# Two half passes over the first two blocks, and x taken from PSUM by column groups

## The chip, the cores and the metric

The kernel runs on one core of a Trainium2 chip. The metric is the device time of one execution in microseconds; the median of three runs of the kernel before is 1110.03.

## The reference

Per batch and head a linear attention with a complex decay runs over 768 positions (B = 4, H = 8, D = 48), and its output goes through two layers of 384 -> 2048 -> 384:

```python
mag = np.sqrt(a_re * a_re + a_im * a_im)
scale = np.minimum(mag, 0.999) / (mag + 1e-06)
for t in range(S):                       # a = (a_re + i a_im) * scale
    S_re = ar * S_re - ai * S_im + k[t] (x) v[t]
    S_im = ar * S_im + ai * S_re         # with the old S_re
    y[t] = q[t] @ S_re
x = y as (B * S, H * D)
x = (h * cos(h)) @ w_out,   h = x @ w_in
out = elu(h) @ w2_out,      h = x @ w2_in
```

The weights arrive as 64-bit floats, and the kernel decodes them on the chip.

## The kernel before, in words

The positions are cut in 6 chunks of 128, and with 4 batches that gives 24 steps; step i is (chunk i // 4, batch i % 4). A step of the attention takes logarithm and angle of the decay (`a1_pre`, `a1_ln`, `a1_lam`, `a1_th`), sums them over the chunk with a triangular product (`p_tri`), makes exponentials, cosine and sine (`a2_exp`, `a2_ph`, `a2_trig`), scales q and k with them (`a2_mag`, `a2_xy`), transposes the two results four heads at a time (`b_tr`), forms masked scores (`b_sc`), y from scores and from the state of the chunks before (`b_y`), and the new state (`b_ds`). y comes out transposed, heads in rows, in one bank of PSUM. `b_out` copies it to SBUF, six DMAs regroup its rows to three full blocks of 128, and `x_split` cuts it into a rounded part (ScalarE) and a rest (GpSimd).

Three steps are one block of 384 columns. The first layer runs 8 blocks of 16 units; a unit is one slice of 128 hidden rows: nine products into h (L467), a chain over ScalarE, VectorE and GpSimd (`chain_a`, `chain_b`, `chain_c`), and nine products that add to the block's three accumulators (L568). The second layer does the same for 8 blocks of the layer's result, with its own weights. A unit's h is formed three units ahead of its last products (LA).

Weights of the first layer: `w_load` brings a slice as 64-bit words, `w_dec` turns it into 32-bit floats (one scaling on ScalarE, L435, three operations on VectorE, L436 to L439), `w_put` splits it (a cast on ScalarE, L452, a subtraction on VectorE, L454). Those of the second layer are decoded during blocks 4 to 6 of the first and stored.

What sets the order: ScalarE executes in the order in which the code emits its instructions. For the other engines a scheduler orders by priority, which starts as the order of emission and is shifted by `prio` (OFF for decoding, OFP for `w_put`, PRI per token). The opening is a written list of tokens, PRO: the attention of steps 0 to 2, parts of the next ones, and R, D, P for loading, decoding and putting one weight. After it the three first units start, and the steps that follow come in eight pieces each (SLOT; a number after the colon is an offset to the step), spread over the units of a block so that a block's three steps are ready before it starts (`need`, `run_pieces`). SP issues all DMAs in one queue. PSUM has eight banks: three accumulators, five working banks (`work`) for everything else.

For the general case the kernel checks bounds of a_re and a_im (`bounds`): for steps 9 and later in `a1_pre`, for the first NDF = 9 in the second layer from a second load.

Of the kernel before, what the change touches and what calls it, by code (L numbers as in the profile page):

```python
# [11 lines left out]
F32 = mybir.dt.float32  # L12
# [18 lines left out]
OFF = (-200, 0)  # L31
# [3 lines left out]
YTA, RHP, CARP = 3, 2, 0  # L35
NDF = 9
# [6 lines left out]
NYT, NXS = 2, 2  # L43
NX, PD = 4, 23
PRO = ('L:0 L:1 L:2 R pre:0 pre:1 V:0 Q:1 V:2 V:1 Q:2 R Q:0 pre:2 TL ln:0 ln:1 ln:2 lam:0 lam:1 lam:2 TT th:0 th:1 th:2 D P TL tri:0 tri:1 exp:0 tri:2 exp:1 exp:2 R ph:1 TT ph:0 ph:2 D trig:0 P trig:1 mag:2 trig:2 mag:0 xy:0 mag:1 R tr0:0 xy:1 xy:2 D R L:3 tr1:0 P sc0:0 tr0:1 D sc1:0 tr1:1 y0:0 tr0:2 R sc1:1 D sc0:1 y1:0 P out:0 ds:0 y0:1 sc0:2 Q:3 y1:1 tr1:2 sc1:2 pre:3 V:3 R out:1 D ds:1 y0:2 P y1:2 ln:3 lam:3 L:4 R out:2 ds:2 xs:1 TT ca:3 pre:4 th:3 tri:3 xs:0 ca:4 D P xs:2 ln:4 L:5 exp:3 lam:4 P ph:3 th:4 trig:3 V:4 mag:3 xy:3 Q:4')
# [8 lines left out]
def tile_kernel(ctx, tc, q, k, v, a_re, a_im, w_in, w_out, w2_in, w2_out, out):  # L54
# [17 lines left out]
    xp = ctx.enter_context(tc.tile_pool(name="xp", bufs=2))  # L72
# [10 lines left out]
    def work():  # L83
        return psW.tile([P, 512], F32, tag="work", name="work")

    def prio(x):
# [20 lines left out]
    Sst = [ap.tile([D2, H, D], F32, name=f"S{b}", tag=f"S{b}") for b in range(B)]  # L107
# [5 lines left out]
                cs=(1, 0), q=(1, 2), k=(1, 3), Y=(2, 0), v=(2, 2), r=(2, 3))  # L113
# [13 lines left out]
    def load(i, names):  # L127
        c, b = steps[i]
        for nm in names:
            t = buf(i, nm, LB[nm]).rearrange("p (h d) -> p h d", h=H)  # L130
            nc.sync.dma_start(out=t, in_=SRC[nm][b, :, c * P:(c + 1) * P, :].rearrange("h t d -> t h d"))
            st[i][nm] = t
# [19 lines left out]
    def a1_pre(i):  # L152
# [7 lines left out]
        e = buf(i, "e")  # L160
        if i >= NDF:
            bounds(i, ar, ai)
        s["L"], s["w"], s["e"] = L, w, e

    def a1_ln(i):
        s = st[i]
        if i >= NB0:
            nc.scalar.preload_act_table_set(LN_SET)  # L168
        ar, e = fl(s["ar"]), s["e"]
# [10 lines left out]
    def a1_lam(i):  # L180
        s = st[i]
        L = s["L"]
        nc.vector.scalar_tensor_tensor(out=L, in0=L, scalar=2.0 * LN_CAP, in1=s["w"], op0=ALU.min,
                                       op1=ALU.subtract)
        if i >= N_NAT:
            s["hi"] = ap.tile([P, 2, HD], F32R, name="lth")
            s["lo"] = ap.tile([P, 2, HD], F32R, name="ltl")
            split(s["hi"][:, 0, :], s["lo"][:, 0, :], L)

    def a1_th(i):  # L190
        s = st[i]
        th = s["th"]
        nc.scalar.activation(out=th, in_=th, func=AF.Arctan, scale=-1.0)
# [14 lines left out]
    def p_tri(i):  # L208
        s = st[i]
        s["Lp"], s["Fp"] = work(), work()  # L210
        if i < N_NAT:
            nc.tensor.matmul(out=s["Lp"][:, 0:HD], lhsT=tri, rhs=s["L"], start=True, stop=True)
            nc.tensor.matmul(out=s["Fp"][:, 0:HD], lhsT=tri, rhs=s["th"], start=True, stop=True)
            return
        for j, ps in ((0, s["Lp"]), (1, s["Fp"])):
            nc.tensor.matmul(out=ps[:, 0:HD], lhsT=tri_r, rhs=s["hi"][:, j, :], start=True, stop=False)  # L216
            nc.tensor.matmul(out=ps[:, 0:HD], lhsT=tri_r, rhs=s["lo"][:, j, :], start=False, stop=True)  # L217

    def a2_exp(i):
# [37 lines left out]
    def a2_mag(i):  # L257
        s = st[i]
        for m, x in (("E", "q"), ("En", "k")):
            nc.gpsimd.tensor_tensor(out=fl(s[x]), in0=s[m], in1=fl(s[x]), op=ALU.mult)  # L260

    def a2_xy(i):
        s = st[i]
        for nm, m, eng in (("X", "q", nc.vector), ("Y", "k", nc.gpsimd)):
# [5 lines left out]
    def b_tr(i, g):  # L270
        s = st[i]
        for nm, on in (("X", "XT"), ("Y", "YT")):
            ps = work()
            for h in range(4):
                nc.tensor.transpose(ps[0:D2, h * P:(h + 1) * P],  # L275
                                    s[nm][:, g * 4 + h].rearrange("p a d -> p (a d)"), ident)
            t = ap.tile([D2, 4, P], F32, name=on, bufs=2 if nm == "X" else NYT)
# [17 lines left out]
    def w64(h):  # L295
        return slice(min(h * D, HD - 64), min(h * D, HD - 64) + 64)

    def b_y(i, g):
# [4 lines left out]
        yp = s["yp"]  # L303
        for pr in range(2):
            gp = g * 2 + pr
            for n in range(2):
                hh = pr * 2 + n
                nc.tensor.matmul(out=yp[n * 64:n * 64 + 64, gp * P:(gp + 1) * P], lhsT=fl(s["v"])[:, w64(g * 4 + hh)],  # L308
                                 rhs=s["AT", g][:, hh, :], start=True, stop=c == 0)
            if c > 0:  # L310
                for n in range(2):
                    hh = pr * 2 + n
                    nc.tensor.matmul(out=yp[n * 64:n * 64 + 64, gp * P:(gp + 1) * P],  # L313
                                     lhsT=fl(Sst[b])[:, w64(g * 4 + hh)], rhs=s["XT", g][:, hh, :],
                                     start=False, stop=True)
# [18 lines left out]

    def b_out(i):
        s = st[i]
        if i < NB0:
            yT = scr[3 * i][:, 2:4, :].rearrange("p a f -> p (a f)")[:, 0:4 * P]
            yT = yT.rearrange("p (a t) -> p a t", a=4)
            xs = buf(i, "E").rearrange("p (a t) -> p a t", a=KT)  # L340
        else:
            yT = ap.tile([P, 4, P], F32, name="yT")
            xs = ap.tile([P, KT, P], F32, name="xs", bufs=NXS)
        nc.scalar.copy(out=yT.rearrange("p a t -> p (a t)"), in_=s["yp"])
        s["xs"] = xs
        dm = nc.sync.dma_start
        dm(out=xs[0:48, :, :], in_=yT[0:48, 0:3, :])
        dm(out=xs[48:96, :, :], in_=yT[64:112, 0:3, :])
        dm(out=xs[96:128, 0, :], in_=yT[0:32, 3, :])
        dm(out=xs[96:112, 1, :], in_=yT[32:48, 3, :])  # L350
        dm(out=xs[112:128, 1, :], in_=yT[80:96, 3, :])
        dm(out=xs[96:128, 2, :], in_=yT[96:128, 3, :])
# [17 lines left out]
    def x_split(i):  # L370
# [3 lines left out]
        split(xh[:, :, sl], xl[:, :, sl], st[i]["xs"])  # L374

    TOK = dict(L=lambda i: load(i, ("ar", "ai")), Q=lambda i: load(i, ("q", "k")), V=lambda i: load(i, ("v",)),
               pre=a1_pre, ln=a1_ln, lam=a1_lam, ca=a1_carry, th=a1_th, sp=a1_sp, tri=p_tri, exp=a2_exp, ph=a2_ph,
               trig=a2_trig, mag=a2_mag, xy=a2_xy, tr0=lambda i: b_tr(i, 0), tr1=lambda i: b_tr(i, 1),
               sc0=lambda i: b_sc(i, 0), sc1=lambda i: b_sc(i, 1), y0=lambda i: b_y(i, 0), y1=lambda i: b_y(i, 1),
               ds=b_ds, out=b_out, xs=x_split,  # L380
               TL=lambda i: nc.scalar.preload_act_table_set(LN_SET),
               TT=lambda i: nc.scalar.preload_act_table_set(TRIG_SET),
# [453 lines left out]
```

## Time and profile before

| | |
|---|---|
| median of three runs | 1110.03 us (1109.04 to 1110.41) |
| the profiled execution's own time | 1111.97 us |
| its span in the trace | 1110.3 us |
| busy: TensorE, ScalarE, VectorE, GpSimd | 1033.3, 768.6, 631.7, 547.8 us |
| mean granted clock of TensorE | 0.97 |

The span is what lies between the first and the last instruction of the trace. The page gives each engine's busy time over all of it; the rows below cut it at the blocks of the first layer. A line number in a row is one of the kernel before; where a helper emits an instruction, it is the helper's line (L146 is the subtraction in `split`). PE is TensorE, DVE VectorE, ACT ScalarE, POOL GpSimd.

### The profile page before, as it was taken

The numbers are of one execution on the slowest core, as the hardware profiler recorded it, in microseconds if no ns is written. First come the engines' busy times: TensorE is split into PE (matmuls) and PEld (weight loads), VectorE is DVE, ScalarE is ACT, GpSimd is POOL, SyncE is SP. The second block draws the span as 40 slices with busy tenths as digits, with TensorE's granted clock in tenths as the row PEclk, the third lists the DMA queues.
The fourth block names the chain that finished last, engine by engine and source line by source line (L and its number), as shares of the span: only waits on it lengthen the run. The fifth ranks groups of instructions, "written<-read, shape, count | busy, mean of one in ns | idle before, by whom it ended". The sixth has DMA issues, their size and how long they took to land.

```text
span 1110.3 us, 18114 instructions
## 1 busy us (share of the span) xinstructions
PE 1033.3 (93%) x6498; PEld 982.2 (88%) x6498; DVE 631.7 (57%) x999; ACT 768.6 (69%) x1492; POOL 547.8 (49%) x471
## 2 busy tenths in 40 slices
PE   2567987999999999899999999999999999999997
PEld 1456877999999999789899899999999999999997
DVE  3867897665574774786887565434333334333332
ACT  6677866777786875776877456876666767666664
POOL 2435565565555573573665346783434344343432
PEclk9778997999999999899999999999999999999999
DMA  9553551232232322654544275320000010100000
GB/s 204 131 145 68 123 130 30 52 64 59 50 62 48 66 51 58 185 136 121 152 125 154 81 190 136 114 65 22 22 23 22 22 43 1 44 1 22 1 22 26
DMA packets 199037, 85.19 MB, mean 77 GB/s; under 512 B 164573, under 2 KB 190745, under 8 KB 198937
## 3 DMA queue, kind: packets, MB, share of 16 engines
q1 hardware_dynamic: 198936, 83.94, 30.0%
q8 instruction: 53, 0.87, 0.3%
q14 instruction: 48, 0.39, 0.1%
HBM read 63.40 MB, written 15.79 MB: 71 GB/s over the span
## 4 chain that ended last, share of the span: by engine, by line
PE 79%; ACT 5%; DVE 3%; issue 1%; POOL 1%; DMA 0%; SPq 0%; ACTq 0%; DVEq 0%; POOLq 0%
PE work L467 34%; PE acc L568 27%; PE work L568 6%; PE work L288 3%; PE work L275 2%; PE work L308 2%; PE work L313 1%; PE work L324 1%; ACT L168 1%; PE work L216 1%; DVE dec L436 1%; DVE dec L437 1%; DVE wt L454 1%; POOL xl L146 0%; PE work L217 0%
## 5 line engine op out<-in xcount | busy, mean ns | idle before, releaser
L467 PE MATMUL work<-xh,wt 128*128 128x384 f32 x1536 | 444.7, 345 | 14.0 <-DVE wt L454 5.2
L146 POOL TENSOR_TENSOR gl<-t,gh 128x384 fp32r<-128x384 f32 x256 | 279.4, 1094 | 297.0 <-ACT gh L145 118.4
L467 PEld LDWEIGHTS work<-xh,wt 128*128 128x128 f32 x1536 | 283.4, 191 | 24.9 <-DVE wt L454 6.9
L467 PE MATMUL work<-xl,wt 128*128 128x384 f32 x768 | 224.2, 339 | 0.1
L524 DVE SCALAR_TENSOR_TENSOR t<-e,t 128x384 f32<-128x384 f32 x128 | 76.6, 598 | 229.8 <-ACT t L523 161.4
L568 PE MATMUL acc<-gh,wt 128*128 128x384 f32 x768 | 201.9, 350 | 0.1
L145 ACT CAST gh<-t 128x384 fp32r<-128x384 f32 x256 | 130.2, 509 | 92.3 <-PE acc L568 58.1
L568 PE MATMUL acc<-wt,gh 128*128 128x384 f32 x512 | 161.8, 334 | 0.0
L467 PEld LDWEIGHTS work<-xl,wt 128*128 128x128 f32 x768 | 143.5, 191 | 0.4 <-POOL xl L146 0.4
L568 PEld LDWEIGHTS acc<-gh,wt 128*128 128x128 f32 x768 | 139.4, 193 | 3.6 <-issue 2.9
L517 ACT ACTIVATE t<-work 128x384 int32<-128x384 f32 x128 | 61.6, 481 | 80.1 <-PE work L467 74.8
L534 DVE TENSOR_TENSOR t<-work,t 128x384 f32<-128x384 f32 x128 | 70.6, 551 | 66.1 <-ACT t L533 65.4
L568 PE MATMUL acc<-gl,wt 128*128 128x384 f32 x384 | 103.2, 340 | 4.4 <-POOL gl L146 4.4
L518 DVE SCALAR_TENSOR_TENSOR t<-t,work 128x384 f32<-128x384 int32 x128 | 69.8, 546 | 51.1 <-ACT t L517 50.2
L568 PEld LDWEIGHTS acc<-wt,gh 128*128 128x128 f32 x512 | 95.3, 188 | 0.0
L521 ACT ACTIVATE t<-work 128x384 f32<-128x384 f32 x128 | 62.8, 491 | 33.3 <-PE work L467 24.9
L568 PE MATMUL work<-wt,gh 128*128 128x384 f32 x256 | 85.5, 334 | 0.0
L533 ACT ACTIVATE t<-t,hpi 128x384 f32<-128x384 f32 x128 | 78.8, 616 | 3.8 <-DVE t L518 3.7
L568 PE MATMUL acc<-wt,gl 128*128 128x384 f32 x256 | 76.4, 334 | 0.0
L568 PEld LDWEIGHTS acc<-gl,wt 128*128 128x128 f32 x384 | 69.7, 190 | 5.5 <-POOL gl L146 5.4
L536 DVE SCALAR_TENSOR_TENSOR t<-work,t 128x384 f32<-128x384 f32 x128 | 71.4, 558 | 4.4
L522 ACT ACTIVATE e<-t 128x384 f32<-128x384 f32 x128 | 67.4, 527 | 4.1
(142 smaller groups left out, 1748.0 us busy)
## 6 DMA issues: line engine op xcount, KB each, us to landing
raw<-in_moe_w_out_dram SPq DMA_DIRECT2D x32, 384.0 KB
raw<-in_moe_w_in_dram SPq DMA_DIRECT2D x16, 384.0 KB
w2f<-dec SPq DMA_DIRECT2D x16, 384.0 KB
raw<-w2f SPq DMA_DIRECT2D x16, 384.0 KB
raw<-in_moe_w_in_dram SPq DMA_DIRECT2D x16, 288.0 KB
x2d<-ev SPq DMA_DIRECT2D x24, 192.0 KB
x2s<-x2d SPq DMA_DIRECT2D x8, 576.0 KB
out_dram<-ev SPq DMA_DIRECT2D x24, 192.0 KB
```

The lines of the kernel that those rows point to most:

```text
L145: nc.scalar.copy(out=hi, in_=x)
L146: nc.gpsimd.tensor_tensor(out=lo, in0=x, in1=hi.bitcast(F32), op=ALU.subtract)
L467: nc.tensor.matmul(out=out_ps, lhsT=a, rhs=b_, start=m == 0, stop=m == n - 1)
L517: nc.scalar.activation(out=ki, in_=h, func=AF.Copy, scale=1.0 / TWO_PI, bias=0.25)
L518: nc.vector.scalar_tensor_tensor(out=t, in0=ki, scalar=-TWO_PI, in1=h, op0=ALU.mult, op1=ALU.add)
L521: nc.scalar.activation(out=t, in_=h, func=AF.Relu, scale=-1.0)
L522: nc.scalar.activation(out=e, in_=t, func=AF.Exp, scale=-1.0)
L524: nc.vector.scalar_tensor_tensor(out=t, in0=e, scalar=1.0, in1=t, op0=ALU.add, op1=ALU.mult)
L533: nc.scalar.activation(out=t, in_=t, func=AF.Sin, bias=hpi)
L534: nc.vector.tensor_tensor(out=t, in0=h, in1=t, op=ALU.mult)
L536: nc.vector.scalar_tensor_tensor(out=t, in0=h, scalar=0.0, in1=t, op0=ALU.max, op1=ALU.add)
L568: nc.tensor.matmul(out=o, lhsT=a, rhs=b_, start=ff == 0 and x == 0, stop=ff == NFF - 1 and x == 2)
```

## The change

1. Units: block 0 and block 1 run slices 0 to 7 in turn, then slices 8 to 15 in turn. At the end of a first half the accumulators are stored to x2d; near the end of the second half they are loaded and added. Weights are paced over 18 units, and the pieces of the steps follow the new order.
2. y in groups of 32 columns: four heads' first or last 32 columns go to the four quarters of the output rows, and the 16 that remain of two heads share a group, padded by zeros, so that y is in PSUM as three full blocks of 128. `x_split` reads PSUM directly, its rest on VectorE. `b_out` and its six DMAs are gone; w_in's rows are loaded in the matching order.
3. `table` writes a load of ScalarE's function table only where the last one differs.
4. Engines: the first five weights are scaled and cast on VectorE (ED); q and k are scaled on VectorE in the first five steps (MG); Y is formed on VectorE in the first three (YG) and evicted on VectorE in all (YTA); the product with a_im is on VectorE always (RHP).
5. All 24 bounds are checked in the second layer (NDF), in its blocks 1 and 2.
6. The token list PRO and the pieces SLOT are rewritten; transposes and their evictions are separate tokens (tr, ev), as are the two prefix products (tl, tf). OFF for the second layer's decoding goes from 0 to -200.

```diff
-OFF = (-200, 0)
+OFF = (-200, -200)
-YTA, RHP, CARP = 3, 2, 0
-NDF = 9
+YTA, RHP, CARP = 0, 0, 0
+NDF = 24
+MG, YG = 5, 3
-PRO = ('L:0 L:1 L:2 R pre:0 pre:1 V:0 Q:1 V:2 V:1 Q:2 R Q:0 pre:2 TL ln:0 ...
+PRO = ('Q:2 L:1 L:0 V:1 L:2 V:0 R Q:0 R pre:1 Q:1 pre:0 ln:0 D pre:2 ln:1 ln:2 lam:0 lam:1 lam:2 tl:0 tl:1 tl:2 exp:0 exp:1 th:0 th:2 P L:3 exp:2 R mag:1 R tf:0 th:1 ph:0 tf:1 ph:1 mag:0 trig:0 xy:0 D tr0:0 tf:2 trig:1 tr1:0 ph:2 ev0:0 ds:0 ev1:0 xy:1 sc0:0 tr0:1 sc1:0 y0:0 tr1:1 trig:2 mag:2 y1:0 ev0:1 xy:2 xs:0 sc0:1 ev1:1 V:2 sc1:1 y0:1 y1:1 tr0:2 tr1:2 ds:1 ev0:2 ev1:2 D D sc1:2 pre:3 P sc0:2 xs:1 y0:2 ln:3 lam:3 y1:2 ds:2 xs:2 D th:3 P tf:3')
-SLOT = ['out:-1 tri:1 pre:2', 'L:3 ln:2 tr0 ph:1 exp:1', 'sc0 xs:-1 tr1 lam:2', 'trig:1 ca:2', 'mag:1 y0 th:2', 'sc1 xy:1 V:2 sp:2', 'Q:2 y1', 'ds']
+SLOT = ['xs:-1 pre:2', 'tl:1 tf:1 exp:1 ph:1 tr0 ev0 ln:2', 'tr1 sc0 y0 lam:2 ev1 trig:1', 'sl:2 L:3 sc1 mag:1',
+        'ca:2', '', 'th:2', 'Q:2 sp:2 y1 xy:1 ds V:2']
+FA, NXB, ED, P0 = 8, 3, 5, 1
+WS = 18
...
+    def table(name):
+        if tab[0] != name:
+            nc.scalar.preload_act_table_set(name)
+            tab[0] = name
...
+    def wide32(t, h):
+        x = (h % 2) * 16
+        return fl(t)[:, h * DP + x:h * DP + x + 32]
+    def rest32(t, h):
+        x = h * DP + (32 if h % 2 == 0 else -16)
+        return fl(t)[:, x:x + 32]
...
+        for kind in range(1 if c == 0 else 2):
+            for j in range(4):
+                h = 4 * g + j
+                a, x = ((V, s["AT", g]), (Spad[b], s["XT", g]))[kind]
+                nc.tensor.matmul(out=yp[32 * j:32 * j + 32, g * P:(g + 1) * P], lhsT=wide32(a, h), rhs=x[:, j, :],
+                                 start=kind == 0, stop=kind == 1 or c == 0)
+        if g == 0:
+            return
+        for kind in range(1 if c == 0 else 2):
+            for n in range(2):
+                for j in range(4):
+                    h = 2 * j + n
+                    a, x = ((V, s["AT", h // 4]), (Spad[b], s["XT", h // 4]))[kind]
+                    nc.tensor.matmul(out=yp[32 * j:32 * j + 32, 2 * P:3 * P], lhsT=rest32(a, h), rhs=x[:, h % 4, :],
+                                     start=kind == 0 and n == 0, stop=n == 1 and (kind == 1 or c == 0))
...
-        split(xh[:, :, sl], xl[:, :, sl], st[i]["xs"])
+        yp = st[i]["yp"][:, 0:HD].rearrange("p (m t) -> p m t", m=KT)
+        nc.scalar.copy(out=xh[:, :, sl], in_=yp)
+        nc.vector.tensor_tensor(out=xl[:, :, sl], in0=yp, in1=xh[:, :, sl].bitcast(F32), op=ALU.subtract)
...
+            trip = cols.rearrange("(m t r) f -> m t r f", t=3, r=32)
+            for m in range(2):
+                for n in range(2):
+                    keep(nc.sync.dma_start(out=raw[64 * n:64 * n + 64, 0, m], in_=trip[2 * m + n, 0:3:2]))
+            keep(nc.sync.dma_start(out=raw[:, 0, 2], in_=trip[:, 1]))
...
-    units = [(0, j, ff) for j in range(NBK) for ff in range(NFF)]
+    segs = [(0, 0, 0, FA), (0, 1, 0, FA), (0, 0, FA, NFF), (0, 1, FA, NFF)]
+    segs += [(0, j, 0, NFF) for j in range(2, NBK)]
+    units = [(l, j, ff) for l, j, a, b_ in segs for ff in range(a, b_)]
...
+    def part_load(j):
+        c0, n = blocks[j][0] * P, ncols(0, j)
+        part[j] = t = stg.tile([P, KT, HD], F32, tag="raw", name="part")
+        nc.sync.dma_start(out=t[:, :, 0:n], in_=x2d[:, :, c0:c0 + n])
...
+                nxt = max([f for a, b_, f in units[:g + LA + 1]]) + 1
+                tgt = min(max(nxt, w00 + (NFF - w00) * (g + 1) // WS), NFF)
                 w_adv(0, tgt + WL)
                 p_adv(0, tgt)
```

## Rows read from the trace of the kernel before

**Rows 1.** Stretches cut at the first layer's blocks: per engine busy us (instructions), clock.

```profile
core 0: us, PE busy (x) PEld busy (x) DVE busy (x) ACT busy (x) POOL busy (x), PEclk, DMA share, GB/s
0.00:76.02 76.02, 32.57 (x209) 23.02 (x209) 46.26 (x62) 49.50 (x84) 23.61 (x25) 0.85 0.77 161
76.02:185.40 109.38, 91.76 (x525) 80.92 (x525) 92.51 (x127) 82.76 (x149) 65.52 (x45) 0.85 0.43 98
185.40:259.50 74.10, 74.10 (x530) 69.50 (x530) 44.89 (x77) 53.98 (x107) 40.17 (x36) 1.00 0.26 53
259.50:335.40 75.90, 75.90 (x541) 71.37 (x540) 47.69 (x80) 55.78 (x111) 44.51 (x40) 1.00 0.27 56
335.40:411.40 76.00, 76.00 (x542) 71.47 (x541) 48.25 (x80) 55.85 (x111) 44.65 (x41) 1.00 0.27 56
411.40:493.60 82.20, 78.78 (x543) 73.80 (x542) 56.98 (x90) 58.24 (x114) 45.68 (x38) 0.96 0.43 114
493.60:574.90 81.30, 77.43 (x528) 72.40 (x527) 63.34 (x96) 60.82 (x119) 46.75 (x40) 0.98 0.50 144
```

**Rows 2.** TensorE's waits, 0 to 200 us: who waited for whom, total, times, longest.

```profile
PE work L212 <- DVE scr L183: 15.1, 1, 15.1
PE work L275 <- DVE scr L267: 8.3, 1, 8.3
...
PE work L467 <- DVE wt L454: 5.2, 2, 2.9
```

**Rows 3.** ScalarE in order of time: start, us, operation, idle time before it.

```profile
64.63 0.57 ACT L344 COPY scr<-work 128x512 f32<-128x512 f32 x1
...
68.36 1.28 ACT L382 ACT_TABLE_LOAD   x1
...
75.45 0.51 ACT L145 CAST xh<-scr 128x384 fp32r<-128x384 f32 x1 [1.18 <-DMA scr<-scr]
```

**Rows 4.** TensorE in order of time, the layer's first product.

```profile
76.02 4.21 PE L467 MATMUL work<-xh,wt 128*128 128x384 f32 x12 [1.97 <-ACT xh L145]
```

**Rows 5.** ScalarE by line, 0 to 76 us: busy, mean ns, idle before.

```profile
L435 ACT ACTIVATE dec<-raw 128x768 f32<-128x768 f32 x7 | 6.4, 909 | 0.0
L452 ACT CAST wt<-dec 128x768 fp32r<-128x768 f32 x6 | 5.0, 827 | 11.1 <-DVE dec L439 11.1
```

**Rows 6.** VectorE by line and shape, 0 to 76.02 us.

```profile
L437 DVE SCALAR_TENSOR_TENSOR dec<-raw,dec 128x768 int32<-128x768 int32 x7 | 6.7, 954 | 0.2
L267 DVE TENSOR_TENSOR scr<-scr 128x768 f32<-128x768 f32 x3 | 6.0, 2017 | 0.0
L436 DVE TENSOR_SCALAR dec<-dec 128x768 int32<-128x768 int32 x7 | 5.8, 823 | 8.4 <-ACT dec L435 8.4
...
L454 DVE TENSOR_TENSOR wt<-dec,wt 128x768 fp32r<-128x768 f32 x6 | 5.7, 953 | 2.1 <-ACT wt L452 2.1
```

**Rows 7.** VectorE by line and shape, 76.02 to 185.4 us.

```profile
L454 DVE TENSOR_TENSOR wt<-dec,wt 128x768 fp32r<-128x768 f32 x11 | 13.7, 1242 | 0.7 <-ACT wt L452 0.7
...
L437 DVE SCALAR_TENSOR_TENSOR dec<-raw,dec 128x768 int32<-128x768 int32 x9 | 11.2, 1246 | 0.1
```

**Rows 8.** VectorE by line and shape, 259.5 to 335.4 us.

```profile
L281 DVE COPY YT<-work 96x512 f32<-96x512 f32 x7 | 4.8, 686 | 1.0 <-PE work L275 1.0
...
L267 DVE TENSOR_TENSOR X<-cs,q 128x768 f32<-128x768 f32 x3 | 2.9, 954 | 0.6 <-POOL gl L146 0.6
...
L177 DVE TENSOR_TENSOR ai<-th,ai 128x384 f32<-128x384 f32 x1 | 0.5, 549 | 0.0
```

**Rows 9.** TensorE in order of time: score products, transposes; two groups of y products.

```profile
233.32 1.06 PE L288 MATMUL work<-XT,YT 96*128 96x128 f32 x8
234.21 0.60 PE L275 MATMUL work<-ident,X 128*96 128x128 f32 x4
...
244.99 0.39 PE L313 MATMUL work<-XT,S 96*64 96x128 f32 x4
245.21 0.39 PE L308 MATMUL work<-AT,v 128*64 128x128 f32 x4
```

More of the change, by code (lines that the diff above doesn't have):

```diff
@@ L106, in tile_kernel @@
     ap = att.enter_context(tc.tile_pool(name="ap", bufs=1))
-    Sst = [ap.tile([D2, H, D], F32, name=f"S{b}", tag=f"S{b}") for b in range(B)]
+    DP = D + 16
+    Spad = [ap.tile([D2, H, DP], F32, name=f"S{b}", tag=f"S{b}") for b in range(B)]
+    Sst = [t[:, :, 0:D] for t in Spad]
+    Vpad = [ap.tile([P, H, DP], F32, name=f"v{x}", tag=f"v{x}") for x in range(NV)]
+    for t in Vpad + Spad:
+        nc.vector.memset(t[:, :, D:DP], 0.0)
     st = [dict() for _ in range(NS)]
@@ L192, in a1_th @@
         th = s["th"]
+        table(TRIG_SET)
         nc.scalar.activation(out=th, in_=th, func=AF.Arctan, scale=-1.0)
@@ L251, in a2_trig @@
         cs = buf(i, "cs")
+        table(TRIG_SET)
         vabs(cs[:, :, 0, :], r.rearrange("p (h d) -> p h d", h=H))
@@ L271, in b_tr @@
         s = st[i]
-        for nm, on in (("X", "XT"), ("Y", "YT")):
-            ps = work()
+        for nm in ("X", "Y"):
+            s[nm, "ps", g] = ps = work()
             for h in range(4):
@@ L388, in token @@
         i += int(o or 0)
-        if name not in ("TL", "TT", "R", "D", "P"):
+        if name not in ("R", "D", "P"):
             if not 0 <= i < NS or (name, i) in done:
@@ L451, in w_put @@
         x = x.rearrange("p (a f) -> p a f", a=2)
-        nc.scalar.copy(out=v[:, :, 0, :], in_=x)
+        if l == 0 and ff < ED:
+            nc.vector.tensor_copy(out=v[:, :, 0, :], in_=x)
+        else:
+            nc.scalar.copy(out=v[:, :, 0, :], in_=x)
         eng = nc.vector if l == 0 else nc.gpsimd
@@ L467, in mm3 @@
             nc.tensor.matmul(out=out_ps, lhsT=a, rhs=b_, start=m == 0, stop=m == n - 1)
-    units = [(0, j, ff) for j in range(NBK) for ff in range(NFF)]
+    segs = [(0, 0, 0, FA), (0, 1, 0, FA), (0, 0, FA, NFF), (0, 1, FA, NFF)]
+    segs += [(0, j, 0, NFF) for j in range(2, NBK)]
+    units = [(l, j, ff) for l, j, a, b_ in segs for ff in range(a, b_)]
+    first = {(l, j, a) for l, j, a, _ in segs} | {(1, j, 0) for j in range(NS // 3)} | {(l, "g", 0) for l in range(2)}
+    last = {(l, j, b_ - 1) for l, j, _, b_ in segs} | {(1, j, NFF - 1) for j in range(NS // 3)} | {(l, "g", NFF - 1) for l in range(2)}
     NB2 = NS // 3
@@ L567, in o_mm_ @@
                 o = acc[m][:, 0:n if l == 0 else HD]
-                nc.tensor.matmul(out=o, lhsT=a, rhs=b_, start=ff == 0 and x == 0, stop=ff == NFF - 1 and x == 2)
+                nc.tensor.matmul(out=o, lhsT=a, rhs=b_, start=(l, j, ff) in first and x == 0,
+                                 stop=(l, j, ff) in last and x == 2)
+    part = {}
+    def part_load(j):
+        c0, n = blocks[j][0] * P, ncols(0, j)
+        part[j] = t = stg.tile([P, KT, HD], F32, tag="raw", name="part")
+        nc.sync.dma_start(out=t[:, :, 0:n], in_=x2d[:, :, c0:c0 + n])
     def evac(l, j):
         n = ncols(l, j)
+        pt = part.pop(j, None) if l == 0 else None
         for m in range(KT):
             t = mp.tile([P, HD], F32, tag="t", name="ev")
-            if m == 1:
+            if pt is not None:
+                nc.vector.tensor_tensor(out=t[:, 0:n], in0=accs[l, j][m][:, 0:n], in1=pt[:, m, 0:n], op=ALU.add)
+            elif m == 1:
                 nc.vector.tensor_copy(out=t[:, 0:n], in_=accs[l, j][m][:, 0:n])
@@ L692, in general @@
                         nc.sync.dma_start(out=out[ds(r0 + m * P, P), :], in_=t)
-    pieces = [p for i in range(NB0, NS + 1) for p in slot(i)]
+    pieces = [p for i in range(P0, NS + 1) for p in slot(i)]
     pos = [0]
@@ L698, in need, with goal @@
         s0, n = blocks[j]
-        return (s0 + n - NB0) * 8 + NX if j else 0
+        return (s0 + n - P0) * 8 + NX if j else 0
+    spans = [(0, FA, 1), (FA, 2 * NFF, 2)] + [(j * NFF, (j + 1) * NFF, j + 1) for j in range(2, NBK - 1)]
+    def goal(x):
+        for a, b_, j in spans:
+            if 2 * a < x <= 2 * b_:
+                d = (b_ - a) * 2 * PD // (2 * NFF)
+                return need(j - 1) + (need(j) - need(j - 1)) * min(x - 2 * a, d) // d
+        return 0
     def run_pieces(upto):
@@ L774, in tile_kernel @@
             if l == 1:
-                if j == 1 and ff < NDF:
-                    c, b = steps[ff]
+                cf = (j - 1) * NFF + ff
+                if 0 <= cf < NDF:
+                    c, b = steps[cf]
                     chk = [xst.tile([P, H, D], F32, tag="chk", name="chk", bufs=2) for _ in range(2)]
@@ L794, in tile_kernel @@
                 chain_a(g + CA)
-            if l == 0 and j + 1 < NBK:
-                run_pieces(lo_ + (hi_ - lo_) * min(2 * ff + 2, PD) // PD)
+            run_pieces(goal(2 * g + 2))
             o_mm(g)
-            if ff == NFF - 1:
+            if (l, j, ff) in last:
                 evac(l, j)
```

127 lines of the change are left out of this document (52 added, 75 removed).

## The prediction

> **What bounds the kernel now.** I read the page first: TensorE is busy for most of the span, so what it waits for, and where, comes before any engine's total. The table of stretches [rows 1] cuts the span at the first product of each block of the first layer. In the third and fourth blocks TensorE never pauses: 75.9 us for 16 units and three attention steps, at full clock. That is the pace that nothing in this change makes shorter, unless the attention products themselves get cheaper. Against it stand three stretches. Before the first product of the layer lie 76.0 us, of which TensorE works 32.6. The first block takes 109.4 us, 33.5 more than the pace, at a mean granted clock of 0.85; the second takes 74.1. The fifth and sixth take 82.2 and 81.3, together 11.6 more than the pace. The waits of TensorE in the first 200 us [rows 2] name VectorE: once for the first inputs, then for a product of the attention, then for decoded weights. So I ask of each part whether it shortens the first 76 us, whether it lets the first two blocks come near 2 x 75.9 = 151.8 us (they take 183.5), and what it costs per step where TensorE is full.
>
> **The change part by part.**
>
> *x straight from PSUM.* Before, a step's y is copied (0.57 us), moved by six DMAs that regroup its rows, cast and subtracted. For the third step the copy starts at 64.63 and the cast at 75.45, having waited for the DMA [rows 3]; the first product of the layer follows at 76.02, released by that cast [rows 4]. With the cast reading PSUM, the cast stands where the copy stood: 64.6 + 0.5 = 65.2, so 10.8 us leave the path. In the steady blocks the same chain lies a whole slot ahead and TensorE is full, so there I count nothing for it, nor for the freed 0.57 us of ScalarE and one subtraction of GpSimd a step. The price is that w_in's rows are loaded in a new order with five DMAs for two; 144 small DMAs on SP's queue fall away for 48 added, 30 for the moved checks and 8 for the partial sums, so SP is not the next bound.
>
> *The y product in groups of 32 columns.* A later step has 32 products instead of 16, two records each: 64 for 32. Of today's 64-wide ones four records pass in 0.22 us, so two go abreast, 0.111 us a pair [rows 9], which is what one record of the full-width score products costs (0.89 us for eight, same rows). If four 32-wide ones go abreast, 64 records take 16 x 0.111 = 1.78 us as 32 do now: cost 0. If only two do, 32 x 0.111, which is 1.78 us more. A step of the first chunk has half of that, so over all there are 20 x 16 + 4 x 8 = 352 groups of four, and the bounds are 0 and 352 x 0.111 = 39.1 us, nearly all of it where TensorE is full. I take 0, since two abreast cost no more than one alone. The Trainium skill speaks against 0: TensorE: Matmul & The Clock Gate, Part 3, "Measured speedup vs the span model", lists 2.38 times for three column tiles, which is 0.79 of three. By an estimate from that, four would cost a quarter more than I take, some 10 us over the kernel, and the sum below would be 1086; no row here has four abreast.
>
> *The opening's order.* ScalarE runs in the written order, and six casts of decoded weights made it stand idle 11.1 us for VectorE's last decoding step; the casts and the scaling are another 5.0 + 6.4 us of its time [rows 5]. Both go to VectorE for the first five weights. Part of the idle time was beside work that had to wait anyway. Bounds 0 and 11.1 us; I take 5, nearer the lower end, because only two of the casts stand between the evictions. Table loads, 1.28 us each on ScalarE [rows 3], are in either written order six after the first one up to the fourth step's arctangent, and two per step later, so "only where it differs" is worth nothing here. VectorE pays [rows 6, 8]: five weights scaled and decoded, 5 x (2 x 0.82 + 2 x 0.95) = 17.7, and three put, 3 x (0.95 + 0.82) = 5.3, against 7 x (0.82 + 2 x 0.95) + 6 x 0.95 = 24.7: 1.7 less. Added are six q and k scalings (nearest row: 0.55 us for the shape), three Y products at 0.95, six evictions at 0.69, three subtractions and two products at 0.55: 13.0. The three X products, now 2.02 us beside GpSimd's Y, go to 0.95 as in the steady block: 3.2 less. That makes 46.3 [rows 1] + 8.1 = 54.4 busy us. It fits before 65, but it can lengthen the chain by anything from 0 to 8.1; I take 3, since part of it is decoding that no step waits for. Opening: -10.8 - 5 + 3 = -12.8, first product at 63.
>
> *Two halves in turn.* Units 0 to 7 of block 0, then 0 to 7 of block 1, then the rest of each. Weights 8 to 15 now have 16 units before their first use where they had 8; in return block 1's three attention steps must be done after 8 units, not 16. Floor: TensorE's 151.8. VectorE's floor: 92.5 + 44.9 = 137.4 now [rows 1], and more: two more puts at 1.24 and two more decodings at 3.3 (1.25 twice [rows 7] and 0.82), two casts at 0.82, four scalings, six subtractions and three products at 0.55, six additions of the partial sums at 0.55: 2.5 + 6.6 + 1.6 + 2.2 + 3.3 + 1.7 + 3.3 = 21.2, so 158.6. VectorE then is the later floor. In block 0 it was busy 92.5 of 109.4 us, 85%, in stretches held up by ScalarE and TensorE in turn; with the work spread evenly I take 95%: 167, a gain of 16.5. Bounds: 151.8 (a gain of 31.7) and 158.6 / 0.85 = 187 (a loss of 3.5). The two stores and two loads of partial sums lie beside 8 units and more.
>
> *Later blocks.* The 24 checks of a_re and a_im move to the second layer: two reductions a step leave VectorE, one subtraction and half a product come, so a block has about 1 us less on VectorE. With the second layer's decoding at a lower priority the 11.6 us lost in the fifth and sixth blocks can shrink. Bounds: 11.6 gained, 3 lost (new order of the queues); I take 5. The third, fourth, seventh and eighth blocks and the second layer: 0, where VectorE has room for the checks, two waits on DMA per unit beside a chain that is fed three units ahead.
>
> *A wait that is new.* The result bank of y is held from the third piece of a slot to the first of the next one, six pieces of eight, instead of four; both score tiles are kept until the last products; and the exponentials are issued in the piece of their prefix product, not one later, so ScalarE with the unit's casts behind it can wait for TensorE. With five working banks this bites only if a bank is short: bounds 0 and what a step costs where TensorE does pause now, in the fifth block, (82.2 - 75.9) / 3 = 2.1 us a step [rows 1]; TensorE shows no idle time at all in the third and fourth blocks, which are nearest, so I take 0.
>
> **Sum.** -12.8 - 16.5 - 5 = -34.3. The profiled execution took 1111.97 us (span 1110.3), 1.9 above the median of 1110.03. From its own time 1077.7; as a median of runs 1075.7.
>
> **Rivals.**
> 1. *Four do not go abreast but two* (slower). Place: each y product, on TensorE where it is full. Price 39.1 us, so 1075.7 + 39.1 = 1114.8. It decides the sign from a group of four at 0.111 + 34.3 / 352 = 0.208 us on. For: twice as many records and no row of four. Against: the pairs. Chance 0.09.
> 2. *Four go abreast with a loss*, a quarter of the way between the bounds: 0.139 us a group, 9.8 us, 1085.5. For: twice the records to start in the same time. Against: two abreast lose nothing. Chance 0.13.
> 3. *VectorE takes the place of the DMA and of the weights*: the opening gains the 10.8 of the DMA less the 8.1 added on VectorE, the two blocks 0, the later ones 3: 1110.0 - 5.7 = 1104.3. For: 158.6 busy us against a floor of 151.8, and the first 8 units also want four or five weights. Against: half the path that I remove is DMA and ScalarE's idle time, not VectorE. Chance 0.15.
> 4. *A bank short*: under a third of that bound, 0.6 us per step over 21 steps, 12.6 us, 1088.3. For: six pieces of eight. Against: the full blocks now. Chance 0.11.
> 5. *Nearer the floors*: opening at 56, the two blocks 157, later blocks 9 better: 20 + 26.5 + 9 = 55.5, 1054.5. Chance 0.14.
> The forecast has the remaining 0.38.
>
> **How the numbers follow.** The range reaches from a little under rival 5, 1050, to 1106, which takes in rivals 2, 3 and 4 and leaves out rival 1 and the far end of 5. About 0.2% (2 us) is what a measurement of this kernel can tell from no change: slower holds most of rival 1 and a little of 3 and 4, 0.10; the same 0.04; faster 0.86.
>
> **What would show it.** Right: first product of the layer at 60 to 66; third block's start at 225 to 235, VectorE over 85% busy between; y's groups of four at 0.11; 75.9 in the third and fourth blocks. The opening is wrong if VectorE or a weight, not the cast of x, releases the first product later than 68. The y part is wrong if the third block takes over 77 with TensorE busy throughout; a short bank shows as idle TensorE in that block. The forecast fails as a whole if the two blocks still take 180.

## The result and the profile after

The changed kernel takes 1121.24 us (1120.23 to 1123.46) beside 1109.53 of the kernel before on the same chip: ratio 1.0111, 95% interval 1.009 to 1.0131. It is slower; 1075.7 was forecast. The profiled execution has a span of 1119.5 us. Its stretches, cut as in [rows 1] (the third row is what the two blocks run after the first half):

```profile
0.00:72.00 72.00, 33.52 (x255) 24.13 (x255) 41.64 (x80) 34.12 (x59) 4.93 (x11) 0.95 0.56 113
72.00:152.50 80.50, 59.63 (x458) 49.84 (x456) 65.99 (x100) 56.09 (x101) 31.25 (x23) 0.87 0.55 121
152.50:261.20 108.70, 100.13 (x753) 92.45 (x754) 85.81 (x131) 81.29 (x156) 55.01 (x43) 0.98 0.36 88
261.20:338.20 77.00, 76.79 (x640) 72.03 (x639) 43.42 (x76) 51.71 (x103) 39.44 (x34) 1.00 0.21 43
...
415.30:491.30 76.00, 75.76 (x634) 70.99 (x633) 55.45 (x91) 56.97 (x111) 42.35 (x34) 1.00 0.38 95
491.30:566.60 75.30, 75.06 (x623) 70.27 (x622) 59.10 (x93) 57.08 (x112) 42.23 (x34) 1.00 0.52 142
566.60:646.80 80.20, 79.41 (x572) 66.97 (x571) 47.75 (x75) 42.79 (x82) 28.47 (x23) 1.00 0.33 99
```

| stretch, us | before | after | forecast |
|---|---|---|---|
| start to first product | 76.0 | 72.0 | 63 |
| blocks one and two | 183.5 | 189.2 | 167 |
| third, fourth | 75.9, 76.0 | 77.0, 77.1 | 75.9 each |
| fifth, sixth | 82.2, 81.3 | 76.1, 75.3 | 5 less together |
| seventh | 69.6 | 80.2 | as before |
| second layer, three blocks | 151.1 | 157.0 | as before |

TensorE's waits up to 72 us (who waited for whom, total, times, longest), against [rows 2]: no cast of x stands in front of the first product, but VectorE does, and a load of v.

```profile
PE work L231 <- DVE scr L197: 22.0, 2, 14.6
PE work L299 <- DVE scr L291: 6.7, 1, 6.7
PE work L342 <- DMA v<-in_v_dram: 5.4, 1, 5.4
```

ScalarE in order of time: the third step's cast of x, against [rows 3]; then the layer's first product on TensorE, against [rows 4]:

```profile
68.67 0.48 ACT L393 CAST xh<-work 128x384 fp32r<-128x384 f32 x1 [6.06 <-PE work L351]
```

```profile
71.98 4.16 PE L495 MATMUL work<-xh,wt 128*128 128x384 f32 x12
```

The cast is done 2.8 us before that product, and what it waited for is y itself. In the chain that ended with that product SP issues without a pause from 0.8 to 24.0 us, and later three landings of DMAs stand in it, each until what waited for it starts (start, us):

```profile
24.04 8.30 DMA raw<-in_moe_w_out_dram
53.02 10.01 DMA raw<-in_moe_w_in_dram
63.08 3.46 DMA v<-in_v_dram
```

One weight's issues in SP's queue, before (first fence) and after (start, us, instruction; x4 is four issues):

```profile
18.97 3.04 SPq L419 DMA_DIRECT2D raw<-in_moe_w_in_dram  x1
22.05 0.47 SPq L420 DMA_DIRECT2D raw<-in_moe_w_in_dram  x1
22.56 0.43 SPq L423 DMA_DIRECT2D raw<-in_moe_w_out_dram  x1
```

```profile
18.59 4.80 SPq L440 DMA_DIRECT2D raw<-in_moe_w_in_dram  x4
23.44 0.55 SPq L441 DMA_DIRECT2D raw<-in_moe_w_in_dram  x1
24.04 0.66 SPq L444 DMA_DIRECT2D raw<-in_moe_w_out_dram  x1
```

Summed over 0 to 155 us, the weights' issues take 56.2 us (72 issues, for 12 weights) where they took 23.6 (45 issues, for 15).

### The profile page after: what moved, and what is told of

The parts are those of the page before. It is cut to its first block, busy times and chain, and to the rows that moved or that the text cites. A ratio compares the mean times of both kernels' runs of the same rounds, so it can differ in the third digit from the quotient of the medians.

```text
span 1119.5 us, 19364 instructions
## 1 busy us (share of the span) xinstructions
PE 1038.6 (93%) x7202; PEld 978.0 (87%) x7202; DVE 642.5 (57%) x1076; ACT 743.5 (66%) x1452; POOL 489.7 (44%) x422
## 4 chain that ended last, share of the span: by engine, by line
PE 72%; ACT 8%; DVE 6%; DMA 6%; SPq 4%; issue 2%; POOL 1%; DVEq 0%; ACTq 0%; POOLq 0%
PE work L495 33%; PE acc L601 24%; PE work L601 5%; PE work L342 2%; ACT L94 2%; PE work L317 2%; PE work L351 2%; SPq L440 2%; PE work L299 1%; DMA raw<-in_moe_w_in_dram 1%; SPq L147 1%; DMA raw<-in_moe_w_out_dram 1%; PE work L361 1%; DMA w<-f_d 1%; ACT XT L308 1%
## 5 line engine op out<-in xcount | busy, mean ns | idle before, releaser
L495 PE MATMUL work<-xl,wt 128*128 128x384 f32 x768 | 227.1, 340 | 0.2 <-POOL xl L162 0.2
L601 PE MATMUL acc<-gh,wt 128*128 128x384 f32 x768 | 194.5, 346 | 3.3 <-ACT gh L161 3.0
L601 PEld LDWEIGHTS acc<-gh,wt 128*128 128x128 f32 x768 | 136.3, 189 | 8.3 <-ACT gh L161 3.9
L291 POOL TENSOR_TENSOR Y<-cs,k 128x768 f32<-128x768 f32 x21 | 48.8, 2324 | 78.2 <-ACT cs L277 30.6
```

The lines of the kernel that those rows point to most:

```text
L291: eng.tensor_tensor(out=t, in0=s["cs"], in1=mm.to_broadcast([P, H, 2, D]), op=ALU.mult)
L495: nc.tensor.matmul(out=out_ps, lhsT=a, rhs=b_, start=m == 0, stop=m == n - 1)
L601: nc.tensor.matmul(out=o, lhsT=a, rhs=b_, start=(l, j, ff) in first and x == 0, stop=(l, j, ff) in last and x == 2)
```

## The experiments

Theory A: SP's queue, with six issues per weight, lengthens the opening and the two blocks. Theory B: eight units are too few to cover the three steps that must be done beside them. Theory C: the steps' own chain sets the first half. The seventh block and the second layer are asked apart. Ratios are to the kernel before, on the same chip. "First half" is the time from the first product to the ninth of the first layer's units in their new order. The time of a stretch is that of one profiled execution; a kernel's executions can lie 10 us apart (e1: 1094.11 to 1104.12).

**1. One DMA for w_in** (e1). It leaves out the new order of w_in's rows, so that they no longer match x's.

```diff
-            trip = ... five DMAs
+            keep(nc.sync.dma_start(out=raw[:, 0], in_=cols.rearrange("(j p) f -> p j f", p=P)))
```

> Changed kernel (1121 us) with w_in's slice of the first layer loaded by one DMA in the plain row order instead of five (so the first layer's sum is formed from rows in the wrong order). Theory A, the queue: the six issues per weight hold SP for 56 of the first 155 us and the steps' small transfers (r_d, the carry, v) wait behind them; then the first product of the layer comes by 67 instead of 72, the first two blocks take about 170 us instead of 189, and the time is about 1098. Theory B, the cover: the half order leaves steps 3 to 5 only 8 units to lie beside; then the two blocks still take over 182 and the time stays at 1113 to 1121.

1102.24 us, .9895 (.9849 to .9941). First product at 57.6, 14.4 sooner; first half 80.8, two blocks 186.5. The five DMAs cost the opening 14.4 us and the first half nothing: A is right for the one and wrong for the other.

**2. Whole blocks** (e2: FA = 16; e5: FA = 16 with one DMA), and 12 units (e14, on e13 below).

> Changed kernel with the first two blocks run whole, one after the other, as before (first half of 16 units, no partial sums); all else as changed. Theory B: steps 3 to 5 get 16 units of cover again, the two blocks come back to 175 to 183 us from 189 and the time to 1107 to 1115. Theory A: the chain is as slow as in the halves and weights are needed sooner, the two blocks take 189 or more and the time is 1121 to 1130.

> Whole blocks (as e2) and one DMA for w_in in the plain order (as e1; rows in the wrong order). It separates the half order from the queue. If the queue made whole blocks slow in e2 (206 us for two), they now take 175 or less, the first product comes at 58, and the time is under 1094, less than the halves with one DMA (1102): then the half order itself is a loss. If whole blocks are bound by the weights on VectorE, which they need in half the time, they stay over 190 and the halves are the better order: 1106 or more.

> The same as the repaired kernel, but the first half has 12 of the 16 units of block 0 (FA = 12) and the second part 20 units in place of 24. If the first half lasts as long as three steps' chain of their own lasts, and units lie beside it for nothing: it stays within 3 us, and the 20 units left are 4 x 4.5 us = 18 us shorter (108.7 us for 24 in the changed kernel): two blocks near 168 us. If each unit's weight costs work on the engines of the steps: between 8 units in 80.5 us and 16 in 132 us lies 6.4 us a unit, so the first half is 26 us longer and the two blocks 5 to 10 us longer than with 8 units.

1135.5 (1.022, 1.0198 to 1.0243): two blocks 205.9. With one DMA 1106.3 (.9968, .9939 to .9997): 194.0 against e1's 186.5. With 12 units 1117.29 (1.0045, 1.0027 to 1.0064): two blocks 203.0 against 193.7. Halves are a gain of 16.7 and 7.5 us (the second is near the spread of executions), so B falls. With 12 units the first half is 27.7 us longer than with 8 and the rest 18.4 shorter: each unit put into the first half costs more there than it saves later, and C, the steps' chain alone, doesn't set it either.

**3. The issues on another engine**, w_in's five DMAs from GpSimd (e6), from ScalarE for three weights (e16) or all (e17; the last two on e3 below).

```diff
-keep(nc.sync.dma_start(out=raw[64 * n:64 * n + 64, 0, m], ...
+keep(nc.gpsimd.dma_start(out=raw[64 * n:64 * n + 64, 0, m], ...     # e16, e17: nc.scalar
```

> Changed kernel, rows right, with the five w_in DMAs of a first-layer weight issued from GpSimd instead of SP. If SP's queue (its order and the time of its issues) is what costs the opening, the first product comes at 58 to 64 instead of 72 and the time is 1106 to 1113. If it is the DMA engines that are slowed by five transfers in place of one, the opening stays at 70 to 73 and the time at 1119 to 1125, or more if GpSimd's own work waits behind its issues.

> The kernel with y at priority 150 (1105.9 us, first product at 72.0), in which the five w_in DMAs of the first three weights are issued by ScalarE in place of SP; those of the later weights stay on SP. If the length of SP's queue alone makes the opening long: 15 of its issues at some .78 us go, 11.7 us, and the first product comes at 60 to 62; the two blocks stay at 191.6 us, so the time is near 1095. If it is the DMAs themselves, or an issue on ScalarE costs as much as on GpSimd (3.3 us each, 50 us): the first product comes at 72 or later, up to 100.

> The same with the w_in DMAs of all the first layer's weights on ScalarE. With cheap issues, and the raw buffers free when ScalarE comes to them: opening near 60, the first half as with one DMA per weight (80.8 us) or a little less, the two blocks 186 to 190, time near 1092. If ScalarE stands at an issue until a raw buffer is free, its steps stand with it: two blocks over 200 us, time over 1105.

e6: 1302.93 (1.1722, 1.1687 to 1.1756), first product at 133.3. GpSimd's waits up to 133 us in it:

```profile
POOL raw L440 <- issue: 75.6, 22, 5.3
POOL raw L441 <- issue: 20.6, 6, 4.6
```

e16: 1104.8 (.9939, .9919 to .996), against 1105.9 for e3; first product at 77.7 where e3 has it at 72.0, two blocks 186.7 against 191.7. e17: 1141.83 (1.0261, 1.0237 to 1.0285), first product at 90.8, two blocks 207.4. ScalarE's first operations in e16:

```profile
0.81 3.13 ACTq L441 DMA_DIRECT2D raw<-in_moe_w_in_dram  x4
3.96 0.56 ACTq L442 DMA_DIRECT2D raw<-in_moe_w_in_dram  x1
5.61 5.28 ACTq L441 DMA_DIRECT2D raw<-in_moe_w_in_dram  x4
10.93 1.77 ACTq L442 DMA_DIRECT2D raw<-in_moe_w_in_dram  x1
12.73 1.28 ACT L172 ACT_TABLE_LOAD   x1 [12.73 <-issue]
```

These ten issues are 10.7 us of ScalarE's time, and its first operation starts at 12.7 (.8 in the changed kernel), so they hold up the engine that makes them. With fifteen issues fewer on SP the opening is not shorter but 5.7 us longer, ScalarE's late start among the reasons. Whether the issues or the transfers behind them make the changed kernel's opening long isn't told apart by these runs. The Trainium skill (DMA: Bandwidth & Descriptors, "Anatomy of one DMA — SWDGE (gpsimd) path") puts most of a DMA's fixed cost in its completion and calls descriptor generation "small, variable". This trace disagrees: 28 issues on GpSimd have 96.2 us in front of them, 3.4 each, on the issuing engine, and the profile shows no wait for that time.

**4. What the first half waits for.** e7: one DMA, x split a piece later. e8: one DMA, Y and the scalings of nine steps on VectorE. e11: e8 without two decoding operations for weights 3 to 8. e15: e8 with Exp or Relu for Sin and Arctan in steps 3 to 6 and 8 units, and no table loads there. e18: both. (All five keep e1's order of rows; e11, e15 and e18 compute other numbers.)

```diff
-SLOT = ['xs:-1 pre:2', 'tl:1 tf:1 exp:1 ph:1 tr0 ev0 ln:2', ...          # e7
+SLOT = ['pre:2', 'tl:1 tf:1 exp:1 ph:1 tr0 ev0 ln:2 xs:-1', ...
-MG, YG = 5, 3                                                            # e8
+MG, YG = 9, 9
+        if l != 0 or plain or not 3 <= ff < 9:                           # e11, ahead of the two operations
+            if g >= FA:                                                  # e15, ahead of table(TRIG_SET)
```

> One DMA for w_in (as e1, rows in the wrong order), and the cast of x moved in the written order from the start of the next step's pieces to the end of the second piece. Theory C, the chain: units 4 to 7 of the first half have a whole step each, and a step is a serial chain of some 17 us because the cast of x, which waits for y, stands ahead of the next step's first operations on ScalarE (6.9 us of waits); moved behind them, the first half takes 72 to 76 us instead of 80.8 and the time is 1094 to 1098. If the chain is bound elsewhere (the operations themselves), the first half stays at 79 to 82 and the time at 1100 to 1104.

> One DMA for w_in (as e1, rows in the wrong order), and q, k scaling and Y on VectorE for the first nine steps instead of five and three. Theory C: Y on GpSimd (2.6 us) stands on a step's chain and on VectorE takes about 1.2, so each of the steps 3 to 8 is 1.4 us shorter, the first half 3 to 6 us, time 1096 to 1099. If VectorE is the bound of the two blocks, its 6 x 1 us more make it longer: 1103 to 1108.

> As e8 (one DMA for w_in, rows in the wrong order; q, k scaling and Y on VectorE for nine steps), and without two of the three decoding operations on VectorE for the weights 3 to 8 (these weights keep wrong bits): 12 operations of about 0.95 us less in the first half, where VectorE is busy 93% in e8. If VectorE is the bound of the first half, its 72.4 us become 60 to 64 and the time about 1085. If the steps' own chain is (ScalarE's order with its table loads), it stays at 70 to 73 and the time at 1092 to 1095.

> The kernel with one DMA per weight and all element products on VectorE (first half 72.4 us), in which steps 3 to 6 and the first 8 units take Exp or Relu in place of Sin and Arctan, so that no table is loaded there: the numbers computed are others, the shapes and the rest of the work the same. Theory of the steps' chain on ScalarE: each of three steps has two loads of 1.28 us and the waits behind them, so the first half is 8 to 11 us shorter, near 62 to 64, and later blocks are the same. If VectorE, 93% busy there, or the weights set the first half: 70 to 73 us, the same. The time follows: near 1084 or near 1092.

> The kernel without table loads in the first half (first half 77.0 us) and also without the last two decoding operations of weights 3 to 8 (1.7 us gained by that alone): the numbers computed are others. If VectorE took ScalarE's place as the bound when the loads went (the chain shows it there), taking 12 operations of .95 us from it now shortens the first half by 7 to 11 us, to 66 to 70. If neither engine's load but the waits between the engines set it: 74 to 77.

| | time, ratio (interval) | first half | VectorE, ScalarE busy in it |
|---|---|---|---|
| e1 | 1102.24, .9895 | 80.8 | 66.2, 56.1 |
| e7 | 1111.9, 1.0004 (.9988 to 1.0019) | 81.1 | |
| e8 | 1093.97, .9834 (.9792 to .9876) | 72.4 | 68.3, 55.7 |
| e11 | 1091.48, .9807 (.9776 to .9838) | 70.7 | 56.0, 56.2 |
| e15 | 1094.76, .9859 (.9824 to .9894) | 77.0 | 68.5, 46.8 |
| e18 | 1087.43, .9785 (.9764 to .9805) | 64.8 | 58.6, 46.2 |

The chain of waits by line, shares of the first half, of the changed kernel, e1 and e15:

```profile
by line: DMA w<-f_d 9.2%; DMA r_d<-E 8.8%; PE work L495 8.0%; ACT L94 6.4%; SPq L440 5.4%; PE work L231 4.9%; issue 4.1%; PE work L299 3.2%; DVE t L550 2.9%; SPq L441 2.4%; DVE t L567 2.3%; DVE dec L464 2.3%; DVE X L291 2.1%; DVE th L214 2.
```

```profile
by line: issue 13.0%; ACT L94 10.9%; POOL Y L291 6.9%; PE work L351 4.9%; DMA raw<-in_moe_w_out_dram 4.6%; PE work L299 4.6%; PE work L342 3.8%; PE work L491 3.6%; POOL ltl L162 3.2%; ACT L L172 2.5%; PE work L231 2.5%; ACT E L248 2.4%; ACT
```

```profile
by line: issue 10.3%; PE work L496 7.7%; DVE dec L465 5.1%; DVE dec L463 4.9%; POOL ltl L162 4.8%; PE work L366 4.8%; DMA raw<-in_moe_w_in_dram 4.5%; PE work L347 4.1%; DVE wt L483 3.7%; DVE t L551 3.3%; DVE t L569 3.1%; PE work L356 3.0%; 
```

What stands first in the chains changes: two small DMAs on SP's queue (the carry and r_d), then ScalarE's table loads (L94) and GpSimd's Y, then VectorE's decoding. From e8, taking 8.9 us of ScalarE's work alone gains nothing (e15's first half is 4.6 longer, 2.7 of it because it starts sooner), 12.3 of VectorE's alone gains 1.7, both gain 7.6. As e8's own executions lie between 1089.55 and 1097.39 us, neither single step is told from none; only e18 is clear, each of its executions (1086.4 to 1089.42) being under the fastest of e8. My expectation that the loads alone bind (62 to 64 us) was wrong; that VectorE takes their place (66 to 70) came out, a little low. Moving x's cast (e7) left the first half as it was.

A rival stands untested: TensorE's granted clock alternates between 1.2 and 2.4 GHz in the first half; its mean there, as a share of 2.4, is .83 in e1, .93 in e8, .90 in e11, .89 in e15 and .97 in e18, and TensorE's busy time falls from 62.9 us in e1 to 53.7 in e18. Whether the clock follows the shorter waits or makes the stretch shorter wasn't taken apart.

**5. Two waits in the opening and at a step's start** (e9: the third step's v in spare scratch, r in another place; e10: the angle carried between chunks in scratch of its own, loaded with the decay).

```diff
-cs=(1, 0), q=(1, 2), k=(1, 3), Y=(2, 0), r=(2, 3))
+cs=(1, 0), q=(1, 2), k=(1, 3), Y=(2, 0), r=(0, 3))                       # e9, and v of step 2 at (2, 2)
-            carry = st[i]["w"][0:1, :]
+            carry = st[i]["w"][0:1, :] if own is None else own           # e10, loaded in L
```

> Changed kernel; only v of the third step has a place of its own (spare scratch) and is loaded with the first loads, so that it doesn't wait for the first step's products. If that wait (TensorE idle 5.4 us at 61 to 67) is what holds the opening on top of the queue, the first product comes at 66 to 67 instead of 72 and the time is about 1116. If the weights on SP or VectorE hold it anyway, it stays at 70 to 72 and the time at 1119 to 1122.

> Changed kernel; only the carried row of steps 4 to 6 has a place of its own (spare scratch) and is loaded with the step's first loads, instead of lying in row 0 of w, where its load must wait for w's last reader. If this new wait (VectorE idle 8.5 us for the carried row, later 0.9, ScalarE 7.0 behind it) holds the first half, 80.5 us become 70 to 75 and the time about 1113. If SP's order and the steps' own chain hold it, the first half stays at 78 to 81 and the time at 1118 to 1122.

e9: 1138.72 (1.0262, 1.0222 to 1.0302), first product 100.4. It made a wait of its own: r now shares its place with X, so X waits for the DMA that still reads r, and TensorE for X. TensorE's and VectorE's waits up to 100 us:

```profile
PE work L311 <- DVE scr L303: 30.5, 1, 30.5
```

```profile
DVE scr L303 <- DMA f_d<-scr: 10.1, 2, 6.6
```

So the wait for v stays untested. e10: 1125.87 (1.012, 1.0087 to 1.0152), first half 85.9 against 80.5: the carry's wait (8.5 us, on VectorE) goes and nothing is gained.

**6. y kept together; decoding's priority** (e3, e4).

```diff
-PRI = {'pre': -60, 'ds': -30, 'trig': 60}
+PRI = {'pre': -60, 'ds': -30, 'trig': 60, 'y0': 150, 'y1': 150}          # e3
-OFF = (-200, -200)
+OFF = (-200, 0)                                                          # e4
```

> Changed kernel with a higher priority for the y products, so that TensorE's order has 12 changes between them and other products in the seventh block instead of 58. If changing between 32-column products and full ones is what makes that block 80.2 us instead of 69.6, it comes back to 70 to 72, the third and fourth lose up to 0.5, and the time is about 1111. If the seventh block is long for another reason (pieces that come late, a bank), it stays at 78 to 81 and the time at 1119 to 1122.

> Changed kernel with the second layer's decoding at its old priority (OFF 0 for -200). If that priority gave the 12 us that the fifth and sixth blocks have gained, they go back to about 81 each, and the second layer's first block, late for its weights now (57.3), goes to 52.5: about +7 us, 1128. If the gain came from the DMAs, checks and GpSimd work that left these blocks, they stay at 75 to 77 and only the 5 us of the second layer's first block come back: about 1116.

e3: 1105.9 (.9948, .9919 to .9977), with the third block at 75.0 and the seventh at 68.2. e4: 1118.2 (1.0061, 1.0037 to 1.0085), fifth and sixth 77.6 and 77.0, the second layer's first two blocks 54.8 and 49.4 against 57.3 and 50.8. TensorE in the seventh block of the changed kernel, in order of time:

```profile
613.83 0.33 PE L601 MATMUL acc<-gh,wt 128*128 128x384 f32 x1
614.00 0.68 PE L601 MATMUL acc<-gl,wt 128*128 128x384 f32 x3
...
615.08 0.62 PE L351 MATMUL work<-AT,v 128*32 128x128 f32 x16
615.52 0.40 PE L351 MATMUL work<-XT,S 96*32 96x128 f32 x6
615.85 0.44 PE L495 MATMUL work<-xh,wt 128*128 128x384 f32 x1
616.22 0.41 PE L351 MATMUL work<-XT,S 96*32 96x128 f32 x2
616.55 0.44 PE L495 MATMUL work<-xh,wt 128*128 128x384 f32 x1
616.92 0.41 PE L351 MATMUL work<-XT,S 96*32 96x128 f32 x2
617.26 0.44 PE L495 MATMUL work<-xh,wt 128*128 128x384 f32 x1
```

One full product and one product of y (two records) alternate, .70 us from one such pair of rows to the next (616.55 - 615.85). In this block TensorE changes 58 times between y's products and others, in e3 12 times. In e3 the 16 stand in one row:

```profile
586.67 0.62 PE L351 MATMUL work<-AT,v 128*32 128x128 f32 x16
587.11 0.62 PE L351 MATMUL work<-XT,S 96*32 96x128 f32 x16
```

**7. The repairs together** (e12: y's priority, e8's engines, e4, e9's v; e13: the same without e9's v).

```diff
-OFF = (-200, -200)
+OFF = (-200, 0)
-MG, YG = 5, 3
+MG, YG = 9, 9
-PRI = {'pre': -60, 'ds': -30, 'trig': 60}
+PRI = {'pre': -60, 'ds': -30, 'trig': 60, 'y0': 150, 'y1': 150}
```

> A version with right results: changed kernel, plus the y products kept together (e3), q, k scaling and Y on VectorE for nine steps (e8), the old priority of the second layer's decoding (e4) and the early v (e9); still five DMAs for w_in. Sum of the single effects on 1121: -15.5 (e3), -7, -3, -5: about 1091. If the effects overlap (the y priority and the decoding priority act on the same blocks) 1095 to 1102.

> The changed kernel with three of the earlier edits together and no new place for v: y at priority 150, all element products of the steps up to 8 on VectorE, decoding of the second layer without its lead in priority. If the costs found so far add (the run with the misplaced v had two blocks of 183.6 us and 839.5 us from its third block on, the changed kernel's first product is at 72): 72 + 183.6 + 839.5 = 1095 us of span, some 1097 us of time, ratio to the kernel before .985 to .99. If the two blocks gained there only because their start was late (work prepared meanwhile): two blocks near 187 to 189, time 1101 to 1105, ratio near .994.

e12: 1126.72 (1.0141, 1.0114 to 1.0168), with e9's wait in it. e13: 1107.46 (.997, .9952 to .9987), first half 84.1, two blocks 193.7: the gains don't add. With five DMAs a weight, moving Y to VectorE shows no gain (e3's first half is 82.1): ScalarE stands 7.5 us for a load of a_re and VectorE 6.6 for the carry:

```profile
DVE th L214 <- DMA w<-f_d: 6.6, 1, 6.6
```

```profile
ACT L L172 <- DMA ar<-in_a_re_dram: 7.5, 1, 7.5
```

Of the kernels that keep the whole computation, e3 and e16 are the fastest, some .5% under the kernel before.

## Why the prediction was wrong

*The opening, forecast -12.8, was -4.0.* The step that x's cast comes off the path held. What failed is the line "so SP is not the next bound": I counted DMAs over the kernel, where those that fell away come late, and not SP's queue in the first 72 us. That term was 0, and five DMAs in place of one measure 14.4 (e1); without them the first product comes at 57.6, 5 us sooner than I forecast. I had also no term for the weights' landings: two of them, 18.3 us, stand in the chain to the first product, and e1's chain has neither. How the 14.4 divides between issues and landings stays open. A wait that I had not listed came too: the third load of v needs one of two buffers, and then stands in that queue until 63.08 us, behind the landing of a w_in (5.4 us of TensorE's time; its own price wasn't separated). VectorE, put at 54.4 us, is busy 41.6, with three weights decoded and two put where I had counted five and three; its +3 and ScalarE's -5 were not tried alone.

*The two blocks, forecast -16.5, were +5.7.* The step that failed is one floor for both: "with the work spread evenly I take 95%". VectorE is busy 66.0 of 80.5 us in the first half (82%) and 85.8 of 108.7 in the rest (79%), where TensorE works 100.1. The 189.2 us lie beyond even my worse bound (187). The work isn't even: three attention steps must be done in eight units, and a step passes in turn through SP's queue, ScalarE, GpSimd and VectorE. No engine is full on average, and a busy share of one tells little there; after Y's move to VectorE (e8, first half 8.4 shorter than e1's) only relief on two engines at once (e18) gave a clear gain, with the clock's part in it open. The two halves themselves are right: whole blocks cost 16.7 more with this queue (e2). What the new engines and piece order alone did to block 0 wasn't tried.

*The later blocks, forecast -5, were -12.2 in the fifth and sixth, and +10.6 in the seventh.* The first is just beyond the bound I gave (11.6); e4 puts 3.3 us of it on the priority, the rest on what left these blocks (checks, six DMAs a step), not taken apart. The second is a cost for which I had no term: I priced y's products by those standing together [rows 9], and not what TensorE's order makes of them. In the seventh block it puts them singly between full products; e3 moves them together and gives back 12.0 us there, 2.0 in the third and .9 in the fourth, which had each lost 1.1.

*The second layer, forecast 0, was +5.8*: e4 gets 3.9 of it back by decoding its weights sooner.

*y four abreast, forecast 0, is right for products that stand together.* Four rows of y in the first half's trace, in order of time:

```profile
131.68 0.43 PE L342 MATMUL work<-AT,v 128*32 128x128 f32 x8
131.92 0.40 PE L342 MATMUL work<-XT,S 96*32 96x128 f32 x8
132.15 0.62 PE L351 MATMUL work<-AT,v 128*32 128x128 f32 x16
132.58 0.62 PE L351 MATMUL work<-XT,S 96*32 96x128 f32 x16
```

16 records start .43 us apart from the next 16 (132.58 - 132.15): .108 for four, the price of a pair before. Rivals 1 and 2 fall with it. The Trainium skill (TensorE: Matmul & The Clock Gate, Part 3, "Measured speedup vs the span model") has 2.38 times for three column tiles; these rows show no loss with four. Rival 4 falls as well: third and fourth blocks show TensorE busy for 76.8 of 77.0 us, so no bank is short. Rival 3 had the right sign of doubt, that other engines eat the gain of the first 250 us, but in the opening the weights' DMAs and not VectorE came first.

## What to carry to other kernels

Count a change's DMAs against the queue in the stretch where they stand, not over the kernel: splitting a load has a price, in issues on the engine that makes them or in the landings that later issues wait for, though its bytes stay the same. A product in small tiles is as cheap as its records standing together; look where the scheduler puts it among full ones before counting it at that price. Where a few serial steps set a stretch, forecast it by a step's chain through all engines, and expect that relief on one engine alone may show nothing.

## What was not expected of the hardware

In the seventh block one full product and one 32-column product (two records) take .70 us in turn. Among their own kind a full product takes .17 (614.00 - 613.83) and two records of y .05 (.43 / 8). The rest, .48 us, is not all for the two changes: a lone product's two records start .13 us apart, where in a row of 16 four start within .02. By e3 a change costs .26 us in all (12.0 for 46 fewer). SP's mean issue of a weight's DMAs rose from .52 to .78 us with six in a row. An issue cost ScalarE 1.1 us (10.7 for ten) and GpSimd 3.4.
